# Tiles 1 and 2 as a seven-product pair for w_out, and DVE work on two units at a time

## The chip, the cores and the metric

The kernel runs on one core of a Trainium2 chip. The metric is device time in microseconds (us) for one execution, the median of several runs. The engines are TensorE (PE, with its weight loads shown apart as PEld), VectorE (DVE), ScalarE (ACT), GpSimd (POOL) and SyncE (SP); SP does no arithmetic, its queue issues most of the DMA transfers.

## The reference

Linear attention for 8 batches and 8 heads of 576 positions feeds a feed-forward layer on 4608 tokens:

```python
q_s = softmax(q, axis=-1); k_s = softmax(k, axis=2)
kv = einsum('bhsd,bhse->bhde', k_s, v)
x  = einsum('bhsd,bhde->bhse', q_s, kv)      # -> (4608 tokens, d_model 512)
g  = softplus(x @ w_in)                      # w_in 512 x 2048
out = g @ w_out                              # w_out 2048 x 512
```

All inputs and outputs are float32. The kernel keeps the accuracy by writing each operand as a sum of two float32r parts, hi and lo, and each product as three matmuls: hi*hi, lo*hi, hi*lo.

## The kernel before

**Tiles and units.** The 4608 tokens are nine tiles of 512. The 2048 columns of the hidden layer are 16 units j of 128. A tile's `w_in` product for a unit is 4 x 3 matmuls of 128x128 weights on 512 columns, its `w_out` product again 4 x 3.

**Tiles alone and tiles in pairs.** Tiles 0 to `SOLO`-1 (0, 1, 2) go alone: `up` (L743 to L745) makes one unit of `x @ w_in`, `softplus` (L752) bends it, `split_g` (L758 on ACT, L761 on DVE) makes hi and lo of it, `down` (L785 to L787) adds its share of `g @ w_out` into four PSUM banks `po0` to `po3`, `finish` stores the tile row by row from SP's queue. The other six tiles go in three pairs p. In a pair, both products are 2x2 block products done with seven block products for eight (the Strassen-Winograd scheme): `pair_unit` (L870 to L872) for `w_in`, on operands that `operand_unit` forms, and `product_out` (L984 to L986) for `w_out`. Seven for eight costs sums and differences elsewhere: sums of blocks of the weights, once, by DVE (`sum_unit`, `sum_out_unit`, one unit s, that is two columns j, at a time; kept in DRAM and fetched again), and differences of g by DVE for each pair (`less_g`, L951), then hi and lo of each of the seven right sides (`split_right`: L964 on ACT, L967 on DVE). Its results are transposed by DVE (L1021) and stored by POOL's queue, eight stores of 64 KB for every 256 columns of a tile (`store`, L1029).

**Order.** Nothing is scheduled at run time. `ORDER` is a written-out string of tokens, and every engine runs its instructions in the order in which the tokens stand: `U` up, `A` softplus, `G`, `H` split_g, `O`, `I` down, `Y` and `y` sums of weights, `C` pair_unit, `t` less_g, `e` split_right, `d` product_out, `R` and `r` fetches from DRAM, `o` the end of a pair, `k` and `q` the attention. SBUF holds some twenty slots of 8 KB a partition (`w0` to `w15`, `spare`, `x0` to `x2`, `qt`). A tile that takes a slot waits until the last reader of the tile before has done, so the table of slots sets waits too. An instruction that waits holds up what stands behind it on its engine; on SP's queue that holds for the fetches.

Of the kernel before, what the change touches and what calls it, by code (L numbers as in the profile page):

```python
# [39 lines left out]
SOLO = 3  # L40
# [4 lines left out]
IN_HOMES = {0: ("spare", "w2"), 1: ("w2", "spare"), 2: ("spare", "w2")}  # L45
# [4 lines left out]
STAGE = ("w1", "w15", "w0", "spare", "w5", "w6", "w7", "w8")  # L50
STAGE_OUT = ("w12", "w13", "w14", "w1", "w12", "w13", "x1", "w3")
# [10 lines left out]
    k1.3.3 S9 M12.1 J9 q1.6 U8 J10 G7 O7 k1.2.4 M14.1 P9 T11 k1.3.4 D3 Q9 k1.2.5 k1.2.6 M11.1 W1 k1.2.7 J11 k1.3.5 P10
    k1.3.6 q1.5 k1.3.7 U9 Q10 J12 D10 A8 P11 Q11 G8 A9 G9 U10 T15 q1.8 q1.7 k1.2.8 q1.9 P12 Q12 k1.2.9 U11 q1.10
    k1.3.8 A10 A11 O8 M13.1 G10 k2.0.0 T14 T13 J13 P13 Q13 x1.0.0 O9 q1.11 D9 J14 G11 O10 W3 D2 D12 M15.1 U12 A12 W0
    U13 x1.0.1 x1.0.2 P14 Q14 J15 D14 A13 O11 x1.0.3 U14 k1.3.9 x1.1.0 G12 P15 D5 x1.0.4 x1.0.5 A14 O12 x1.1.1 x1.1.2
    x1.1.3 G13 G14 Q15.1 P0 x1.2.0 x1.2.1 x1.2.2 O13 x1.2.3 U15 x1.1.4 x1.1.5 x1.3.0 L2 x1.3.1 x1.3.2 D4 Q0.1 k2.1.0
    x1.3.3 x1.2.4 x1.2.5 x1.3.4 D0 P1 Q1.1 x1.3.5 U16 A15 O14 D1 q2.0 q2.1 G15 k2.0.1 Y0.0 Y0.2 A16 G16 U17 U18 A17
    k2.1.1 U19 k2.0.2 k2.0.3 A18 D7 q2.2 q2.4.1 k2.1.2 k2.0.4 k2.0.5 U20 k2.1.3 k2.1.4 k2.1.5 O15 G17 A19 A20 k2.1.6
    k2.0.6 n n O16 Y0.1 G18 Y1.0 q2.6 q2.8 k2.0.7 k2.1.7 k2.1.8 U21 A21 Y1.2 k2.2.0 Y0.3 U22 O17 G19 k2.1.9 q2.3 D6
    Y1.1 k2.0.8 Y1.3 O18 G20 k2.0.9 Y3.0 k2.3.0 O19 A22 G21 O20 G22 k2.3.1 Y3.1 k2.2.1 Y3.2 Y0.4 k2.2.2 q2.5 Y2.0 Y2.1  # L70
    O21 D8 O22 k2.2.3 k2.3.2 k2.3.3 k2.3.4 k2.3.5 k2.2.4 q2.7 L3 D15 Y4.0 U23 k2.2.5 Y2.2 Y2.3 k2.3.6 k2.2.6 q2.9 A23
    H1.7.0 H1.7.1 k2.2.7 k2.3.7 U24 A24 Y2.4 Y2.5 q2.10 U25 Y4.2 O23 U26 H1.8.0 k2.2.8 k2.2.9 x2.0.0 Y1.4 H1.8.1 A25
    q3.0 x2.0.1 x2.0.2 q3.1 q3.12 H1.9.0 x2.0.3 q2.11 Y3.3 n k3.0.0 Y2.6 O24 D13 Y2.7 U27 Y3.4 k2.3.8 H1.9.1 x2.0.4
    x2.0.5 x2.2.0 k2.3.9 x2.1.0 x2.1.1 Y1.5 Y4.1 Y3.5 Y4.3 O25 A26 H1.10.0 Y4.4 n Y0.5 k3.1.0 Y3.6 A27 U28 A28 x2.1.2
    Y1.6 H1.11.0 H1.10.1 x2.1.3 O26 Y2.8 Y3.7 H1.12.0 U29 q3.2 Y6.0 q3.3 H1.11.1 x2.2.1 x2.1.4 x2.1.5 x2.3.0 D11 O27
    Y0.6 Y0.7 H1.12.1 A29 U30 k3.0.4 k3.0.5 k3.1.4 x2.2.2 q3.5 k3.1.5 Y4.5 x2.2.3 Y1.7 O28 x2.3.1 q3.4 x2.3.2 q3.6
    R0.0 H1.13.0 A30 H1.14.0 U31 Y3.8 Y4.6 x2.3.3 A31 q3.7 Y0.8 H1.13.1 L4 O29 H1.14.1 q3.8 x2.2.4 Y6.1 q3.13 R0.1
    x2.2.5 R0.2 x2.3.4 x2.3.5 k3.0.6 y0.0 y0.1 q3.9 H1.15.0 y0.2 y0.3 H1.15.1 k3.1.6 k3.0.7 k3.0.8 U32 A32 n n q4.0
# [1166 lines left out]
```

## Time and profile before

| | us |
|---|---|
| three runs | 811.52, 811.63, 814.35 |
| median | 811.63 |
| profiled execution | 812.18 |
| its span, first to last instruction | 810.1 |
| PE busy in the span | 801.4 |
| DVE, ACT, POOL busy | 623.6, 513.9, 115.1 |

"Busy" is the time in which an engine works on at least one instruction. Matmuls overlap, so the time of one (0.39 us) is longer than the distance from one to the next; PE's pace is read from the starts in the timeline. Windows give the busy time of each engine in a stretch of the span, the waits say which engine waited for which instruction, and the chain of waits follows the end of the program back to its start.

### The profile page before, as it was taken

How to read it: one execution, taken by the hardware profiler on the slowest of the kernel's cores; microseconds unless marked ns; L12 is line 12 of the kernel's file. 1: busy time of each engine (PE TensorE's matmuls, PEld its weight loads, DVE VectorE, ACT ScalarE, POOL GpSimd, SP SyncE). 2: the span in 40 equal slices, each digit the busy share in tenths (PEclk: the TensorE clock that was granted, in tenths of full speed). 3: DMA queues.
4: the chain of work that ended last, by engine and by line, in shares of the span. 5: the costliest groups of instructions: out<-in, count | busy, mean ns of one | idle time of the engine just before them, and what ended most of it. 6: DMA issues, size and time to landing. Idle time of an engine off the chain costs nothing.

```text
span 810.1 us, 12075 instructions
## 1 busy us (share of the span) xinstructions
PE 801.4 (99%) x4244; PEld 656.3 (81%) x4244; DVE 623.6 (77%) x1027; ACT 513.9 (63%) x860; POOL 115.1 (14%) x219
## 2 busy tenths in 40 slices
PE   8999999999999999999999999999999999999997
PEld 7578888888888888888888888888888888888885
DVE  8889884689899998878599998757798932228884
ACT  4999954545674846586887566676676632436552
POOL 1320022001010100100010021430000111600017
PEclk9999999999999999999999999999999999999999
DMA  9976736665798799898588477973756664839845
GB/s 344 376 266 234 267 131 234 215 214 208 253 342 310 246 371 322 315 307 300 185 266 246 146 216 269 279 248 116 240 176 192 195 208 167 264 128 291 268 118 92
DMA packets 114492, 193.74 MB, mean 239 GB/s; under 512 B 8000, under 2 KB 90176, under 8 KB 104192
## 3 DMA queue, kind: packets, MB, share of 16 engines
q1 hardware_dynamic: 111168, 186.67, 67.8%
q0 software_dynamic: 2944, 6.04, 3.7%
q8 instruction: 34, 0.56, 0.3%
q10 hardware_dynamic: 320, 0.26, 0.1%
q14 instruction: 26, 0.21, 0.1%
HBM read 149.95 MB, written 42.99 MB: 238 GB/s over the span
## 4 chain that ended last, share of the span: by engine, by line
PE 88%; DVE 4%; POOL 3%; ACT 1%; DMA 1%; issue 1%; POOLq 0%; ACTq 0%
PE po L984 6%; PE po L985 6%; PE po L986 6%; PE po L870 6%; PE po L871 5%; PE po L872 5%; PE ph L743 5%; PE po L787 5%; PE po L785 5%; PE ph L744 5%; PE ph L745 4%; PE po L786 4%; PE ph L870 3%; PE ph L872 3%; PE ph L871 3%; PE ph L984 3%
## 5 line engine op out<-in xcount | busy, mean ns | idle before, releaser
L1029 POOL DMA_DIRECT2D out<-w x92 | 59.4, 653 | 292.3 <-DVE w L1021 287.6
L743 PE MATMUL ph<-x,w 128*128 128x512 f32 x164 | 65.0, 396 | 0.0
L785 PE MATMUL po<-w,g_hi 128*128 128x512 f32 x164 | 64.7, 395 | 0.0
L787 PE MATMUL po<-w,g_lo 128*128 128x512 f32 x164 | 64.1, 391 | 0.5 <-DVE g_lo L761 0.5
L744 PE MATMUL ph<-x,w 128*128 128x512 f32 x164 | 64.0, 390 | 0.0
L786 PE MATMUL po<-w,g_hi 128*128 128x512 f32 x164 | 63.9, 390 | 0.0
L745 PE MATMUL ph<-x,w 128*128 128x512 f32 x164 | 63.9, 390 | 0.0
L967 DVE TENSOR_TENSOR g_lo<-w,g_hi 128x512 fp32r<-128x512 f32 x74 | 49.4, 682 | 16.8 <-ACT g_hi L964 16.7
L964 ACT CAST g_hi<-w 128x512 fp32r<-128x512 f32 x74 | 45.5, 620 | 19.6 <-PE po L985 16.5
L951 DVE TENSOR_TENSOR w<-w,w 128x512 f32<-128x512 f32 x72 | 48.4, 681 | 3.0 <-ACT w L904 2.0
L870 PE MATMUL po<-w,x 128*128 128x512 f32 x112 | 44.3, 395 | 0.0
L872 PE MATMUL po<-w,x 128*128 128x512 f32 x112 | 43.6, 390 | 0.0
L871 PE MATMUL po<-w,x 128*128 128x512 f32 x112 | 43.6, 389 | 0.0
L487 POOL PARTITION_ALL_REDUCE mx<-mx x20 | 19.1, 954 | 172.0 <-DVE mx L484 169.8
L964 ACT CAST w<-w 128x512 fp32r<-128x512 f32 x52 | 31.9, 620 | 17.9 <-PE po L985 13.9
L893 DVE TENSOR_TENSOR w<-po,w 128x512 f32<-128x512 f32 x24 | 16.5, 686 | 34.1 <-PE po L872 34.0
L761 DVE TENSOR_TENSOR g_lo<-g,g_hi 128x512 fp32r<-128x512 f32 x46 | 31.4, 688 | 13.7 <-ACT g_hi L758 13.5
L967 DVE TENSOR_TENSOR w<-w,w 128x512 fp32r<-128x512 f32 x52 | 35.2, 683 | 6.1 <-ACT w L964 5.9
L758 ACT CAST g_hi<-g 128x512 fp32r<-128x512 f32 x46 | 28.3, 620 | 15.6 <-PE po L786 12.8
L752 ACT ACTIVATE g<-ph 128x512 f32<-128x512 f32 x48 | 28.6, 601 | 14.7 <-PE ph L745 14.2
L787 PEld LDWEIGHTS po<-w,g_lo 128*128 128x128 f32 x164 | 30.8, 188 | 7.9 <-DVE g_lo L761 1.4
L484 DVE TENSOR_REDUCE mx<-kvt 128x128 f32<-128x640 f32 x28 | 36.8, 1324 | 0.1
(392 smaller groups left out, 2371.3 us busy)
## 6 DMA issues: line engine op xcount, KB each, us to landing
x<-sums SPq DMA_DIRECT2D x24, 1024.0 KB, 5.6
kvt<-in_kv SPq DMA_DIRECT2D x30, 512.0 KB, 6.3
kept<-w SPq DMA_DIRECT2D x15, 1024.0 KB, 7.5
w<-kept SPq DMA_DIRECT2D x13, 1024.0 KB, 7.9
x<-sums_out SPq DMA_DIRECT2D x44, 256.0 KB, 5.0
w<-kept SPq DMA_DIRECT2D x36, 256.0 KB, 4.8
x<-kept SPq DMA_DIRECT2D x36, 256.0 KB, 4.4
w<-sums_out SPq DMA_DIRECT2D x36, 256.0 KB, 5.4
```

Of the source, the lines that this page charges most:

```text
L743: nc.tensor.matmul(ph, lhsT=w_hi, rhs=x_hi, start=h == 0, stop=False)
L744: nc.tensor.matmul(ph, lhsT=w_lo, rhs=x_hi, start=False, stop=False)
L745: nc.tensor.matmul(ph, lhsT=w_hi, rhs=x_lo, start=False, stop=h == HP - 1)
L785: nc.tensor.matmul(po, lhsT=g_hi[:, ms], rhs=w_hi, start=j == 0, stop=False)
L786: nc.tensor.matmul(po, lhsT=g_hi[:, ms], rhs=w_lo, start=False, stop=False)
L787: nc.tensor.matmul(po, lhsT=g_lo[:, ms], rhs=w_hi, start=False, stop=j == NJ - 1)
L870: nc.tensor.matmul(ph, lhsT=w_hi, rhs=x_hi, start=c == 0 and i in (0, 4), stop=False, **more)
L871: nc.tensor.matmul(ph, lhsT=w_lo, rhs=x_hi, start=False, stop=False, **more)
L872: nc.tensor.matmul(ph, lhsT=w_hi, rhs=x_lo, start=False, stop=c == 1, **more)
L964: nc.scalar.copy(ring[p, i, s][0], right_of(p, i, s))
L967: engine.tensor_tensor(out=lo, in0=right_of(p, i, s), in1=hi.bitcast(F32), op=ALU.subtract)
L984: nc.tensor.matmul(bank, lhsT=w_hi, rhs=hi, start=begin, stop=False, **more)
```

## The change

`SOLO` falls from 3 to 1, so there are four pairs. The new pair 0 is tiles 1 and 2. It takes part in the seven-product scheme for `w_out` only: its `w_in` products are still made by `up`, 16 units for each tile, with g of both tiles kept in SBUF (slots `g0.1.*`, `g0.2.*`) until its `w_out` products run. The weights' hi and lo parts are kept in DRAM, and the parts for `up` of tiles 1 and 2 are fetched again two columns at a time (`fetch_w`, `part_in`).

DVE and ACT work on two units per instruction in three places: differences of g (`less_g`), hi and lo of the right sides (`split_right`, with views from `two_of`), and the sums of blocks of the weights (`sums_unit`, which takes the place of `sum_unit` and `sum_out_unit`; for `w_in` the parts are fetched from DRAM by `fetch_parts` first). The ring that holds hi and lo has six units in place of four. Slots are given out by a table, `HOMES`; `ORDER` is a new string. Tiles 1 and 2 are stored as the other pairs are, by POOL.

```diff
-SOLO = 3
+SOLO = 1
 ORDER = """
-    k1.0.3 k1.0.4 U0 k1.1.0 k1.0.5 J4 U1 A0 k1.0.6 x0.2.3 k1.0.7 x0.2.4 O0 J3 P2 Q2 x0.0.3 ...
+    k1.0.3 k1.0.4 U0 k1.0.5 k1.1.0 A0 x0.3.3 P2 x0.1.3 J4 x0.0.3 x0.2.3 J3 P3 Q2 M5 x0.0.4 ...
...
+HOMES = """
+    q0:qt kv2:x0 kv3:x2 raw0:w0 raw1:w1 raw2:w2 raw3:w3 qT:w15 x0:x1 raw4:w4 raw5:w5 ...
+    x1.0:w4 parts0:x2 parts14:w0 parts15:qt x1.1:w5 q2:w6 y0:spare y1:w11 g0.1.0:x2 ...
+    T3.2:x1 T2.2:w13 T4.2:w1 end1.3:x2 sum17:w9 g6.1.0:w7 sum18:spare g5.0.0:w3 ...
+    sum22:x2 g6.1.1:x0 sum21:spare g5.0.1:w9 g6.0.1:w6 g5.1.1:w0 ...
...
+    def slot(key, shape, dtype=F32R):
+        return wp.tile([P] + list(shape), dtype, name=HOMES[key])
...
+    gg = const.tile([P, 2, 2, TOK], F32R, name="gg")
...
+    def fetch_w(s):
+        again[s] = slot(f"again{s}", (2, 2, DM))
+        for z in range(2):
+            nc.sync.dma_start(out=again[s][:, z].bitcast(F32), in_=kept[2 * s + z][:, :, 0])
+
+    def fetch_parts(u):
+        for i in range(2):
+            pulled[u, i] = slot(f"{'YH'[i]}{u}", (2, 4, 2 * P))
...
+    def part_in(j, i):
+        return again[j // 2][:, j % 2, i] if j // 2 in again else parts[j][:, i, 0]
...
+    def sums_unit(u, side, keeps):
...
+        def whole(z=None, engine=nc.vector):
+            if side == 0:
+                engine.tensor_tensor(out=y, in0=y, in1=split[0].bitcast(F32), op=ALU.add)
+                return
...
         def add(out, a, b, op, engine=nc.vector):
-            engine.tensor_tensor(out=y[:, out], in0=y[:, a], in1=y[:, b], op=op)
+            engine.tensor_tensor(out=y[:, :, out], in0=y[:, :, a], in1=y[:, :, b], op=op)
...
     def softplus(t, j, ph):
-        soft[t, j] = tp.tile([P, TOK], F32, name="g", bufs=3)
+        if t:
+            if ("up", t, j // 4) not in state_g:
+                state_g["up", t, j // 4] = slot(f"g0.{t}.{j // 4}", (4, TOK), F32)
+            soft[t, j] = state_g["up", t, j // 4][:, j % 4]
+        else:
+            soft[t, j] = tp.tile([P, TOK], F32, name="g", bufs=3)
         nc.scalar.activation(soft[t, j], ph, AF.Softplus)
...
+    def two_of(t, j):
+        z, k = j % 2, j // 2 % 4
+        if ("up", t, j // 4) in state_g:
+            return state_g["up", t, j // 4].rearrange("p (k z) n -> p k z n", z=2)[:, :, z]
+        return state_g[t, z, j // 8][:, k:k + 2]
...
     def less_g(p, name, s, engine=nc.vector):
-        b11, b12, b21, b22 = (soft.get((t, 2 * s + z)) for z in range(2) for t in (ta, tb))
+        out, a, b = (two_of((ta, tb)[int(n[1]) - 1], 2 * s + int(n[0]) - 1) for n in (out, a, b))
         engine.tensor_tensor(out=out, in0=a, in1=b, op=ALU.subtract)
...
     def split_right(p, i, s, part, engine=nc.vector):
+            place = n // 2 % 3 + 3 * (p == NP - 1 and 0 <= n - 6 * NS < 4)
+            if place == 0:
+                t = gg
...
+            ring[p, i, s, "two"] = [t[:, :, k] for k in range(2)]
+            nc.scalar.copy(ring[p, i, s, "two"][0], right_of(p, i, s))
```

In the rows below, a name is the tile's slot and a number that the builder gives it; `x`, `w` or `spare` is the slot's family.

First PE, tile 1's first unit in `w_out` before: four banks, three matmuls each.

```order
L785 MATMUL po_1437<-w_1185,g_hi 128x512
L786 MATMUL po_1437<-w_1185,g_hi 128x512
L787 MATMUL po_1437<-w_1185,g_lo 128x512
L785 MATMUL po_1438<-w_1185,g_hi 128x512
L786 MATMUL po_1438<-w_1185,g_hi 128x512
L787 MATMUL po_1438<-w_1185,g_lo 128x512
L785 MATMUL po_1439<-w_1185,g_hi 128x512
L786 MATMUL po_1439<-w_1185,g_hi 128x512
L787 MATMUL po_1439<-w_1185,g_lo 128x512
L785 MATMUL po_1440<-w_1185,g_hi 128x512
L786 MATMUL po_1440<-w_1185,g_hi 128x512
L787 MATMUL po_1440<-w_1185,g_lo 128x512
```

And the new pair's first product of `w_out` in the changed kernel, the first unit s (`gg` is the first place of the ring, `w_2112` the block of weights fetched from DRAM):

```order
L980 MATMUL ph_2218<-gg,w_2112 128x512
L981 MATMUL ph_2218<-gg,w_2112 128x512
L982 MATMUL ph_2218<-gg,w_2112 128x512
L980 MATMUL ph_2222<-gg,w_2112 128x512
L981 MATMUL ph_2222<-gg,w_2112 128x512
L982 MATMUL ph_2222<-gg,w_2112 128x512
```

Before, two tiles and two units were four such groups of 12 matmuls, 48 in all; now they are seven groups of 6, that is 42.

Second DVE, in the first pair's `w_out` before (L967 a lo part, L951 a difference of g, L893 and L897 of the next pair's `w_in`, L677 of the attention):

```order
L967 TENSOR_TENSOR g_lo_3431<-w12_3160,g_hi_3430 128x512
L951 TENSOR_TENSOR w15_3608<-w15_3608,x1_3606 128x512
L897 TENSOR_TENSOR w3_3756<-po2_3669,g_3604 128x512
L677 TENSOR_TENSOR q_lo_3797<-att1_108,q_hi_3796 128x512
L893 TENSOR_TENSOR w0_3574<-po3_3758,w0_3574 128x512
```

And in the new pair's `w_out` in the changed kernel (L944 a difference, L963 the lo part, L493 the maximum of the attention's k):

```order
L963 TENSOR_TENSOR gg_106<-x0_1714,gg_106 128x2x512
L963 TENSOR_TENSOR w4_2161<-w5_1805,w4_2161 128x2x512
L944 TENSOR_TENSOR w5_1805<-w5_1805 128x2x512
L963 TENSOR_TENSOR w10_2245<-w8_1937,w10_2245 128x2x512
L944 TENSOR_TENSOR x2_1368<-w5_1805,x2_1368 128x2x512
L944 TENSOR_TENSOR w8_1937<-w8_1937 128x2x512
L686 TENSOR_TENSOR q_lo_2333<-att1_102,q_hi_2332 128x512
L493 TENSOR_REDUCE mx_2377<-kvt_2257 128x128
```

Each instruction now covers two units, 1024 elements a partition.

Third POOL in the changed kernel, where the pair of tiles 3 and 4 is stored (`x2_4598` and `w0_4239` hold its transposed results, L496 is the maximum across partitions, L467 to L470 fill a k tile):

```order
L1026 DMA out_0<-w0_4239 32x16x32 x4
L1026 DMA out_0<-x2_4598 32x16x32 x12
L467 MEMSET kvt_4763 64x2x64
L468 MEMSET kvt_4763 64x2x65
L470 MEMSET kvt_4763 128x10
L496 ISA mx_4785<-mx_4783 128x128
L1026 DMA out_0<-w0_4239 32x16x32 x8
L1026 DMA out_0<-x2_4598 32x16x32 x4
L1026 DMA out_0<-w0_4239 32x16x32 x4
```

And SP's queue there: `x2_4995` takes the slot that `x2_4598` leaves, and holds the sums of weights for the next pair's seventh unit of `w_in`.

```order
L403 DMA w14_3995<-kept12_1299 128x2x512
L415 DMA x2_4995<-sums0_6_3589 128x2048
L403 DMA w14_3995<-kept14_1419 128x2x512
L471 DMA kvt_5026<-in_kv 128x8x128
L475 DMA kvt_5026<-in_kv_tail 64x2x128
L415 DMA spare_5077<-sums0_7_3839 128x2048
```

Before, the slots that the stores of a pair emptied were written next by ACT or DVE; here one is filled by a fetch, which stands in SP's queue ahead of the others.

## Rows read from the trace of the kernel before

**Rows 1.** The page: busy time by engine, and PE's granted clock by slice.

```profile
PE 801.4 (99%) x4244; PEld 656.3 (81%) x4244; DVE 623.6 (77%) x1027; ACT 513.9 (63%) x860; POOL 115.1 (14%) x219
...
PEclk9999999999999999999999999999999999999999
```

**Rows 2.** Waits of PE, whole span: total us, times, longest.

```profile
PE ph L1186 <- DVE ident L268: 3.0, 1, 3.0
PE po L1044 <- DVE w L1037: 0.5, 1, 0.5
PE po L787 <- DVE g_lo L761: 0.5, 2, 0.4
```

**Rows 3.** Timeline of PE: start us, us of one, instruction.

```profile
121.94 0.40 PE L743 MATMUL ph<-x,w 128*128 128x512 f32 x1
122.17 0.39 PE L744 MATMUL ph<-x,w 128*128 128x512 f32 x1
...
123.99 0.39 PE L743 MATMUL ph<-x,w 128*128 128x512 f32 x1
```

**Rows 4.** DVE by form: shape and count | busy us, mean ns | idle before.

```profile
L951 DVE TENSOR_TENSOR w<-w,w 128x512 f32<-128x512 f32 x72 | 48.4, 681 | 3.0 <-ACT w L904 2.0 <-ACT w L900 0.7
L400 DVE TENSOR_TENSOR w<-w 128x512 f32<-128x512 f32 x13 | 8.7, 683 | 0.0
L409 DVE TENSOR_TENSOR w<-w 128x1024 fp32r<-128x1024 f32 x7 | 8.5, 1214 | 0.9 <-ACT w L406 0.9
L403 DVE TENSOR_TENSOR w<-w 128x256 f32<-128x256 f32 x28 | 11.6, 418 | 0.3
L1021 DVE STREAM_TRANSPOSE w<-w 128x512 f32<-128x512 f32 x23 | 16.1, 703 | 2.3 <-ACT w L1004 2.1
```

**Rows 5.** ACT by form, the same columns.

```profile
L964 ACT CAST g_hi<-w 128x512 fp32r<-128x512 f32 x74 | 45.5, 620 | 19.6 <-PE po L985 16.5 <-PE ph L985 1.4 <-DVE g_lo L967 0.8
L406 ACT CAST w<-w 128x1024 fp32r<-128x1024 f32 x7 | 7.3, 1048 | 0.0
```

**Rows 6.** Windows: length, PE, PEld, DVE, ACT, POOL busy (count), PEclk, DMA share, GB/s.

```profile
200.00:250.00 50.00, 49.72 (x291) 40.70 (x290) 44.99 (x77) 31.93 (x56) 3.70 (x14) 1.00 0.83 294
250.00:300.00 50.00, 49.64 (x299) 41.07 (x298) 45.24 (x80) 31.82 (x52) 6.50 (x16) 1.00 0.82 297
300.00:350.00 50.00, 50.00 (x261) 41.47 (x260) 41.13 (x67) 31.99 (x58) 3.27 (x8) 1.00 0.92 316
400.00:450.00 50.00, 50.00 (x273) 40.98 (x272) 47.47 (x80) 40.23 (x75) 3.11 (x11) 1.00 0.80 248
450.00:500.00 50.00, 50.00 (x229) 41.79 (x228) 48.28 (x76) 27.42 (x51) 7.53 (x10) 1.00 0.60 187
```

**Rows 7.** Timeline of POOL: start us, us, instruction [idle before, releaser].

```profile
490.57 1.06 POOL L487 PARTITION_ALL_REDUCE mx<-mx  x1 [7.53 <-DVE mx L484]
...
517.61 0.70 POOL L487 PARTITION_ALL_REDUCE mx<-mx  x1 [3.87 <-DVE mx L484]
518.19 6.41 POOL L1029 DMA_DIRECT2D out<-w  x10
...
536.07 0.66 POOL L1029 DMA_DIRECT2D out<-w  x1 [1.37 <-DMA out<-w]
...
790.80 15.38 POOL L1029 DMA_DIRECT2D out<-w  x24 [7.55 <-DVE w L1021]
```

**Rows 8.** Chain of waits, 505 to 545 us: start us, us, what.

```profile
521.39 6.03 DMA out<-w
...
530.26 5.04 DMA out<-w
535.30 0.59 ACT w L890
...
539.32 0.50 ACT po L882
539.87 0.50 PE po L870
```

**Rows 9.** POOL by form, and DVE's idle time behind it.

```profile
L519 DVE TENSOR_TENSOR kvt<-kvt,mx 128x640 f32<-128x640 f32 x20 | 16.3, 818 | 4.0 <-POOL mx L487 3.9
...
L487 POOL PARTITION_ALL_REDUCE mx<-mx x20 | 19.1, 954 | 172.0 <-DVE mx L484 169.8 <-PE ph L872 1.7 <-PE ph L986 0.6
```

**Rows 10.** DMA: issues, KB each, median us from issue to landing.

```profile
x<-sums SPq DMA_DIRECT2D x24, 1024.0 KB, 5.6
...
out<-w POOLq DMA_DIRECT2D x92, 64.0 KB, 4.1
...
out<-w SPq DMA_DIRECT2D x2, 128.0 KB, 3.0
```

**Rows 11.** Timeline at the end: PE's last product, the last issues.

```profile
804.06 0.39 PE L986 MATMUL po<-x,spare 128*128 128x512 f32 x1
804.48 0.75 DVE L1037 TENSOR_SCALAR w<-po 128x256 f32<-128x256 f32 x2 [4.10 <-PE po L986]
...
805.79 0.93 SPq L1052 DMA_DIRECT2D out<-w  x2
```

More of the change, by code (lines that the diff above doesn't have):

```diff
@@ L62 @@
[L62 to L66, printed above, removed]
@@ L203 @@
+"""
+HOMES = dict(entry.split(":") for entry in HOMES.split())
 assert START[-1] == NT
@@ L349, in split_w @@
         if part == 0:
-            parts[k] = wp.tile([P, 2, 2, DM], F32R, name=f"w{(k - 1) % NJ}" if k != UNSPLIT % NJ else "spare")
+            parts[k] = slot(f"parts{k}", (2, 2, DM))
         hi, lo = (parts[k][:, i].rearrange("p z n -> p (z n)") for i in range(2))
@@ L387, in fetch_sums @@
         s = n % NS
-        sums_w[s] = xp.tile([P, 2, 4, 2 * P], F32R, name=f"x{2 - 2 * (n % 2)}")
-        nc.sync.dma_start(out=sums_w[s].bitcast(F32), in_=kept_sums[s])
-    def sum_unit(s):
-        f = wp.tile([P, 2, 4, 2 * P], F32R, name=STAGE[s])
-        y = f[:, 1].bitcast(F32)
-        old = parts[2 * s + 1], parts[2 * s]
-        def whole_w(z, engine=nc.vector):
-            hi, lo = (old[z][:, i, 0].bitcast(F32) for i in range(2))
-            engine.tensor_tensor(out=y[:, 2 * z:2 * z + 2].rearrange("p a n -> p (a n)"), in0=hi, in1=lo, op=ALU.add)
+        t = slot(f"sum{n}", (2, 4, 2 * P))
@@ new lines, in fetch_sums @@
+        sums_w[s] = t[:, 0], t[:, 1]
+        nc.sync.dma_start(out=t.bitcast(F32), in_=kept_sums[s])
+    def sums_unit(u, side, keeps):
+        y = (pulled[u, 0] if side == 0 else slot(f"y{u}", (2, 4, 2 * P))).bitcast(F32)
+        split = [pulled[u, 1]] if side == 0 else []
+        def whole(z=None, engine=nc.vector):
+            if side == 0:
+                engine.tensor_tensor(out=y, in0=y, in1=split[0].bitcast(F32), op=ALU.add)
+                return
+            hi, lo = (parts[4 * u + z][:, i, 1].bitcast(F32) for i in range(2))
+            first = 2 * (z % 2)
+            out = y[:, z // 2, first:first + 2].rearrange("p a n -> p (a n)")
+            engine.tensor_tensor(out=out, in0=hi, in1=lo, op=ALU.add)
@@ new lines, in high, with low, keep @@
+            if side:
+                split.append(slot(f"h{u}", (2, 4, 2 * P)))
+            nc.scalar.copy(split[0], y)
+        def low(engine=nc.vector):
+            split.append(slot(f"{'Yy'[side]}l{u}", (2, 4, 2 * P)))
+            engine.tensor_tensor(out=split[1], in0=y, in1=split[0].bitcast(F32), op=ALU.subtract)
+            if side == 0:
+                for z in range(2):
+                    sums_w[2 * u + z] = split[0][:, z], split[1][:, z]
+        def keep(z):
+            t = keeps[2 * u + z] = dram.tile([P, 2, 4, 2 * P], F32, name=f"sums{side}_{2 * u + z}")
+            for i, f in enumerate(split):
+                nc.sync.dma_start(out=t[:, i], in_=f[:, z].bitcast(F32))
@@ L449, in tile_attn_ffn, with kv_load @@
+        steps = (((1, 0, 1, ALU.add), (0, 2, 0, ALU.subtract), (2, 1, 2, ALU.subtract), (3, 3, 2, ALU.subtract)),
+                 ((3, 1, 3, ALU.add), (1, 0, 1, ALU.subtract), (0, 3, 0, ALU.subtract), (2, 2, 0, ALU.subtract)))[side]
+        return [lambda *e, a=a: add(*a, *e) for a in steps] + [
+            high, low, lambda: keep(0), lambda: keep(1)
+        ] + [lambda *e, z=z: whole(z, *e) for z in range(4)]
     KVW = 2 * D + 1
-    def kv_load(b, h, engine=nc.gpsimd, queue=nc.sync, pool=kp, tag="kvt", shape=(P, NCH + 1, 2, KVW)):
-        t, w = pool.tile(list(shape), F32, name=tag), KVW if b else 2 * D
+    def kv_load(b, h, engine=nc.gpsimd, queue=nc.sync):
+        wide, w = not b and h >= 2, KVW if b else 2 * D
+        t = slot(f"kv{h}", (HP * TOK,), F32) if wide else kp.tile([P, NCH + 1, 2, KVW], F32, name="kvt")
@@ L1064, in tile_attn_ffn @@
     kv_order = [(b, h) for b in range(B) for h in range(HP)]
[L1065 to L1072 removed]
+    loaded, ahead = {}, [0]
     def kv_prefetch(**place):
```

489 lines of the change are left out of this document (215 added, 274 removed).

## The prediction

> **What bounds the kernel now.** I read four views in this order. The page's busy times: PE works 801.4 of the 810.1 us, DVE comes next with 77%, and PE's granted clock is full in every slice [rows 1]. But matmuls overlap, so a busy PE says little by itself; the timeline gives the pace. From the start at 121.94 to that at 123.99 lie nine 128x512 matmuls, 0.228 us each, although one lasts 0.39 us [rows 3]; over the whole trace I take 0.2275. Third, the waits: all that the view finds for PE is one wait of 3.0 us at the start, 0.5 us at the end and 0.5 us twice summed in the middle [rows 2]. The reader is to see that after the start PE issues one matmul after the other and hardly ever waits. Fourth, the windows, for how near the others are: DVE is busy 48.28 and 47.47 of 50 us between 400 and 500, and PE loses nothing there; between 200 and 300 DVE has 45 of 50 and PE loses 0.28 and 0.36 us [rows 6]. So **PE's issue bounds the kernel**, and DVE stands right behind it. A matmul less is a gain as long as DVE keeps up.
>
> **PE, what goes.** Before, tiles 1 and 2 need 2 x 16 x 12 = 384 matmuls in `down`. The new pair needs 7 products x 8 units s x 6 = 336. Counted in the built programs, 128x512 matmuls fall from 3152 to 3104, and no other form changes: 48 x 0.2275 = **10.9 us** [rows 3]. All of it lies on the path, since PE hardly waits. That the change does not do what it says is excluded by this count.
>
> **DVE, what is added.** Merging saves little: two 512-element instructions last 2 x 0.68 = 1.37 us and one of 1024 lasts 1.214 [rows 4], but neighbours on DVE overlap by 0.048 us each (the durations of all 1029 instructions sum to 673, DVE is busy 623.6), so a merged pair gains 0.1 us. What is new is pair 0: differences, more lo parts and eight transposes. By form, with durations of [rows 4]: 512-element tensor_tensor 500 to 188 (-312 x 0.683 = -213.1), 1024 from 61 to 221 (+160 x 1.216 = +194.6), 256 from 64 to none (-26.9), sums of 2x256 none to 32 (+21.9), transposes +8 (+5.6), four more adds (+2.7), and twelve of 2048 elements, a form that the trace does not have. From 512 to 1024 an instruction grows by 0.533 us, so 2.28 us is my estimate for 2048, +27.4; ends: 2.0 and 2.43 (two of 1024). Sum +12.2; with 160 instructions fewer the overlap shrinks by 7.7, so DVE goes from 623.6 to **643.5 us**, from 77% to 80.5% of a shorter span.
>
> The mean hides the place. I laid DVE's instructions against PE's in the order of the built program and summed both by these durations. Between 100 and 450 us of PE's work DVE had 306 us of work before; it has **339 us of 350** now, 96.8%, because `up` of two tiles in a row, pair 0's differences and all sums of weights fall there. In its fullest part, 200 to 280 us of PE's work, DVE has 4.8 us more than PE; the fullest part before had 3.8 more. So DVE must be kept at 96.8% for 350 us where it showed 97% for 100 us [rows 6]. If it holds 96%, this stretch takes 339/0.96 = 352.8 us, so PE waits **2.8 us**; that is the value I take, near the two windows. The ends: nothing if it holds 97%, and 25 us at the 90% of the windows between 200 and 300 [rows 6], which I hold for far off, since DVE there was not asked for more.
>
> **A rule weighed.** The all-reduce on POOL took 0.70 us once and 1.06 another time [rows 7], and DVE idled 3.9 us behind twenty of them [rows 9]. The Trainium skill, "SBUF — State Buffer", Who interferes with whom, says that a DVE instruction with two SBUF inputs keeps a GpSimd instruction that reads SBUF out for as long as it lasts. By that rule these all-reduces wait up to 1.2 us instead of 0.7 for a merged instruction, and DVE's idle time grows by 3.9 x (1.216/0.683 - 1) = 3.0 us in the very stretch that has none to spare: the sum below would be 807.1. The trace shows the longer times, not what they hang on.
>
> **ACT.** Casts of 512 fall from 300 to 100 (-200 x 0.62), 112 of 1024 come (+112 x 1.05), 16 of 1024 go, eight of 2048 come (estimate 1.9 from the two rows), two copies and two table loads: -4 us of 513.9 [rows 1, 5]. It stays at 64%; cost nothing, hidden under PE.
>
> **DMA and SP's queue.** SP issues 494 transfers for 406; bytes go from 192.9 to 199.2 MB. Between 50 and 250 us of PE's work the order issues 15 to 16 MB per 50 us, some 310 GB/s. The chip moved 294 to 316 GB/s for 150 us with the DMA share at 0.82 to 0.92, and PE lost 0.6 us there [rows 6]. In the order a refetched `w_in` part is issued 8 to 35 us of PE's work ahead of its first matmul, blocks of weights 4 us or more as before, against landings of about 5.6 us for a megabyte [rows 10]. I take nothing; if the cover fails, one late megabyte costs 2 to 5 us.
>
> **The added wait.** `x2_4995`, sums for the next pair's `w_in`, goes into the slot that the stores of tiles 3 and 4 empty. SP's queue stands at this fetch until POOL's stores from `x2_4598` have landed; behind it wait a `w_in` part and the next k tile, and PE's matmul on `x2_4995` stands right after it. Before, such a backlog ran 24 stores in 536.73 - 518.19 = 18.5 us, 0.77 us each [rows 7], landings took 5.0 to 6.0 us, and ACT's copy came late by it, with PE right behind [rows 8]. Now: all-reduce 0.7, twelve stores 9.2, landing 5.5, the fetch 5.6 [rows 10] make 21.0 us, and between the all-reduce and the matmul lie 20.0 us of PE's work. **1.0 us** of wait; ends 0 (stores at 0.64 us, landing 4.1: 18.1 us) and 4.
>
> **The end.** Before, POOL's last 24 issues run to 806.18 [rows 7], 1.9 us behind PE's last matmul at 804.3, and land at 810.1. In the new order POOL's last issue comes by the same 0.64 us a store 0.9 us behind it, so the end passes to SP's two stores, issued till 806.7 and landing after 3.0 [rows 10, 11]: 809.7. **0.4 us** less.
>
> **Sum.** Against the profiled span, 810.1 - 10.9 + 2.8 + 1.0 - 0.4 = 802.6. The median of the runs is 811.63, 1.5 us over that span (the profiled run's own time is 812.18), so the median will be **804.1 us**.
>
> **The rivals.** (a) **DVE takes the gain back.** The price goes by one number, the share at which DVE can be kept from 100 to 450 us: 95% costs PE 6.5 us and gives 807.8, 93% costs 14 and gives 815.6. For it: in the rows DVE idles behind ACT and PE (3.0 us before L951 [rows 4]), and a merged instruction starts only when both units are there. Against it: 97% in [rows 6], and a ring of six units for four. This ends within 0.5% of before. (b) **Slower**, the same mechanism past its point: below 92.8% the stretch grows by more than 15 us and the time passes 815.7. At 92% it is 811.6 - 10.9 + 18.2 + 1.0 - 0.4 = 819.5. (c) **The lock of the all-reduce**: 807.1 by the rule above, as a mechanism of its own. (d) **DVE costs nothing**: it holds 97% and the fetch is not late, 811.63 - 10.9 - 0.4 = 800.3; for it speaks that PE's loss between 400 and 500 was nil.
>
> **How the numbers follow.** 0.5%, about what a measurement of this kernel can tell from no change, is 4.1 us: faster is below 807.6, slower above 815.7. Forecast, 802 to 806: 0.48. (d), 799.5 to 802: 0.18. (c), 806 to 807.6: 0.10. (a), 807.6 to 815.7: 0.17. (b): 0.07. Faster is 0.76, no change 0.17, slower 0.07. The range goes from 800.0 to 810.0: it leaves out the lower edge of (d), (b), and the upper part of (a), not quite 0.2 in all.
>
> **What will show it.** PE's 128x512 matmuls still 0.2275 us apart; PE's waits, about 4 us more, on DVE's lo parts and differences (L963, L944) between 140 and 490 us; DVE at 96% or more in the windows there; one wait of PE on L872, or of SP, at the fetch of `x2` near 535 us; twelve DVE instructions of 2048 elements at 2.28 us. I am wrong if DVE stays under 94% in those windows while PE waits for it, if PE waits for DMA landings between 100 and 300 us, or if the 48 matmuls are gone and the span is not shorter by more than 5 us.

## The result, and the profile after

| | before | after |
|---|---|---|
| median, us (four runs each) | 812.99 (811.52 to 814.62) | 804.97 (804.63 to 805.22) |
| span of the profiled execution, us | 810.1 | 802.8 |
| matmul records | 4244 | 4196 |

The ratio is 0.9901, 95% interval 0.9875 to 0.9926: faster by 8.0 us, 1.0%. The forecast was 804.1, its range 800.0 to 810.0; by the span it was 802.6, and 802.8 is measured. The sum, though, is right by luck in one part: two errors in it cancel, and that is what the experiments are about.

The page of the kernel after (answers to [rows 1]):

```profile
PE 794.0 (99%) x4196; PEld 647.0 (81%) x4196; DVE 645.7 (80%) x867; ACT 514.8 (64%) x768; POOL 138.1 (17%) x251
...
PEclk9999999999999999999999999999999999999999
```

PE's waits, whole span, after (answers to [rows 2]: total us, times, longest):

```profile
PE ph L1175 <- DVE ident L282: 3.0, 1, 3.0
PE ph L872 <- ACT ph L882: 0.7, 1, 0.7
PE att L692 <- DVE q_lo L686: 0.6, 1, 0.6
PE po L1041 <- DVE g L1034: 0.5, 1, 0.5
```

There is no wait on DVE's lo parts or differences (L963, L944), where I had put 2.8 us, and none at the fetch of `x2`, where I had put 1.0. Two short waits that I had not foreseen stand in their place. The windows after (answers to [rows 6], same columns) show DVE's load:

```profile
100.00:225.00 125.00, 125.00 (x673) 103.49 (x672) 109.88 (x160) 91.74 (x135) 13.07 (x25) 1.00 0.86 295
225.00:314.00 89.00, 89.00 (x506) 73.34 (x505) 86.64 (x110) 53.94 (x79) 12.69 (x29) 1.00 0.86 259
314.00:450.00 136.00, 135.34 (x706) 111.13 (x705) 125.99 (x156) 95.61 (x152) 21.77 (x44) 1.00 0.85 269
```

DVE is busy 109.9 + 86.6 + 126.0 = 322.5 of the 350 us, 92%, and for the 89 us of the new pair's `w_out` 97.3%; PE loses nothing in these 89.

So 10.9 us of matmuls went, PE waited hardly more than before, and yet the span is only 7.3 shorter. The missing part shows in the timeline, at the end of the last product (the columns of [rows 3]):

```profile
795.17 0.39 PE L982 MATMUL po<-w,w 128*128 128x512 f32 x1
795.40 0.39 PE L980 MATMUL po<-w,w 128*128 128x512 f32 x1
795.62 0.39 PE L981 MATMUL po<-w,w 128*128 128x512 f32 x1
795.85 0.39 PE L982 MATMUL po<-w,w 128*128 128x512 f32 x1
796.08 0.40 PE L980 MATMUL po<-gg,w 128*128 128x512 f32 x1
796.31 0.40 PE L981 MATMUL po<-gg,w 128*128 128x512 f32 x1
796.55 0.40 PE L982 MATMUL po<-gg,w 128*128 128x512 f32 x1
796.78 0.40 PE L980 MATMUL po<-gg,w 128*128 128x512 f32 x1
797.01 0.40 PE L981 MATMUL po<-gg,w 128*128 128x512 f32 x1
797.25 0.40 PE L982 MATMUL po<-gg,w 128*128 128x512 f32 x1
```

Matmuls on slots start (796.08 - 795.17)/4 = 0.2275 us apart, those on `gg`, the first place of the ring, (797.25 - 796.08)/5 = 0.234. No engine waits and the clock is full, so no view of waits names it. Over the whole trace, the 636 matmuls with `gg` as moving operand (the 512 columns that stream through) or as weights (the 128x128 block that stays) go at 0.2333 us on average, all other 128x512 ones at 0.2275.

### The profile page after: what moved, and what is told of

It is laid out like the page before. It is cut to its first block, busy times and chain, and to the rows that moved or that the text cites. A ratio compares the mean times of both kernels' runs of the same rounds, so it can differ in the third digit from the quotient of the medians.

```text
span 802.8 us, 11782 instructions
## 1 busy us (share of the span) xinstructions
PE 794.0 (99%) x4196; PEld 647.0 (81%) x4196; DVE 645.7 (80%) x867; ACT 514.8 (64%) x768; POOL 138.1 (17%) x251
## 4 chain that ended last, share of the span: by engine, by line
PE 93%; DVE 3%; DMA 1%; issue 1%; ACT 1%; SPq 0%; DVEq 0%; ACTq 0%
PE po L980 9%; PE po L981 9%; PE po L982 9%; PE po L872 6%; PE po L873 6%; PE po L874 6%; PE ph L752 5%; PE ph L754 5%; PE ph L753 5%; PE ph L980 4%; PE ph L981 4%; PE ph L982 4%; PE ph L872 4%; PE ph L873 3%; PE ph L874 3%; PE att L544 2%
## 5 line engine op out<-in xcount | busy, mean ns | idle before, releaser
L960 ACT CAST w<-w 128x1024 fp32r<-128x1024 f32 x50 | 52.2, 1049 | 33.7 <-PE po L981 18.7
L1026 POOL DMA_DIRECT2D out<-x x60 | 38.6, 651 | 201.0 <-DVE x L1018 198.2
L963 DVE TENSOR_TENSOR w<-w,w 128x1024 fp32r<-128x1024 f32 x50 | 60.8, 1221 | 8.3 <-ACT w L960 8.1
L944 DVE TENSOR_TENSOR w<-w,w 128x1024 f32<-128x1024 f32 x46 | 55.7, 1218 | 3.7 <-DMA w<-kept 2.6
L496 POOL PARTITION_ALL_REDUCE mx<-mx x20 | 20.4, 1018 | 179.7 <-DVE mx L493 178.5
L1026 POOL DMA_DIRECT2D out<-w x64 | 41.5, 656 | 56.1 <-DVE w L1018 56.0
L980 PE MATMUL po<-w,w 128*128 128x512 f32 x128 | 50.4, 393 | 0.0
L981 PE MATMUL po<-w,w 128*128 128x512 f32 x128 | 49.9, 390 | 0.0
L873 PE MATMUL po<-w,w 128*128 128x512 f32 x128 | 49.9, 390 | 0.0
L982 PE MATMUL po<-w,w 128*128 128x512 f32 x128 | 49.8, 389 | 0.0
L960 ACT CAST gg<-w 128x1024 fp32r<-128x1024 f32 x33 | 34.6, 1050 | 20.9 <-PE po L981 8.5
L893 DVE TENSOR_TENSOR x<-po,x 128x512 f32<-128x512 f32 x12 | 8.3, 692 | 49.3 <-PE po L874 49.3
L963 DVE TENSOR_TENSOR gg<-w,gg 128x1024 fp32r<-128x1024 f32 x33 | 40.3, 1222 | 5.5 <-ACT gg L960 5.4
L872 PE MATMUL po<-w,w 128*128 128x512 f32 x110 | 43.1, 392 | 0.0
L874 PE MATMUL po<-w,w 128*128 128x512 f32 x110 | 42.8, 389 | 0.0
L493 DVE TENSOR_REDUCE mx<-kvt 128x128 f32<-128x640 f32 x28 | 36.7, 1324 | 5.2 <-DMA kvt<-in_kv_tail 5.1
L752 PE MATMUL ph<-w,w 128*128 128x512 f32 x98 | 39.4, 402 | 0.0
L753 PE MATMUL ph<-w,w 128*128 128x512 f32 x98 | 38.2, 390 | 0.0
L754 PE MATMUL ph<-w,w 128*128 128x512 f32 x98 | 38.2, 389 | 0.0
L467 POOL MEMSET kvt<- 64x128 f32 x28 | 5.7, 203 | 164.0 <-PE att L544 44.9
L873 PE MATMUL ph<-w,w 128*128 128x512 f32 x80 | 31.2, 390 | 0.0
L980 PE MATMUL po<-gg,w 128*128 128x512 f32 x76 | 30.2, 397 | 0.0
```

The source lines that it names most:

```text
L752: nc.tensor.matmul(ph, lhsT=w_hi, rhs=x_hi, start=h == 0, stop=False)
L753: nc.tensor.matmul(ph, lhsT=w_lo, rhs=x_hi, start=False, stop=False)
L754: nc.tensor.matmul(ph, lhsT=w_hi, rhs=x_lo, start=False, stop=h == HP - 1)
L872: nc.tensor.matmul(ph, lhsT=w_hi, rhs=x_hi, start=c == 0 and i in (0, 4), stop=False, **more)
L873: nc.tensor.matmul(ph, lhsT=w_lo, rhs=x_hi, start=False, stop=False, **more)
L874: nc.tensor.matmul(ph, lhsT=w_hi, rhs=x_lo, start=False, stop=c == 1, **more)
```

## Experiments: why matmuls on `gg` are slow

`gg` is new: one constant tile of 8 KB a partition, laid out behind a 4-byte tile, in place of four small ones. My first theory was its address, 32 bytes past a multiple of 64.

**e1_gg_at_64**

```diff
+    gg = const.tile([P, 2, 2, TOK], F32R, name="gg")
     one = const.tile([P, 1], F32, name="one")
-    gg = const.tile([P, 2, 2, TOK], F32R, name="gg")
```

> The changed kernel with one line moved: the tile gg is laid out ahead of the 4-byte tile one, so that it begins at byte 25728 of a partition, a multiple of 64, and no longer 32 bytes past one; every other large tile stays where it was, and no instruction changes. In the trace of the changed kernel the 636 matmuls of 128x512 that read gg, as moving operand or as weights, start 0.2333 us apart and the others mostly 0.2267. Theory A, the place of gg costs this: with it moved, those matmuls go at 0.2267 us, 636 x 0.0066 = 4.2 us go, 805.0 becomes 800.8 (bounds 800.2 to 801.6). Rival B, it is what gg is (a tile that ACT and DVE write while PE reads its other half): pace and time stay, 805.0, within 0.5. Rival C, the pace changes but DVE is the bound where gg is read (DVE 97% busy from 225 to 314 us): PE waits for DVE instead and less than half of it comes, 803 to 805.

804.84 us, and moving reads of `gg` still 0.2333 us apart. Only its reads as weights went down, to 0.2294. **e2_before_at_32** moved everything in the kernel before by 32 bytes:

```diff
-        first = const.tile([P, 1], F32, name="first")
+        first = const.tile([P, 9], F32, name="first")[:, 0:1]
```

> The kernel before with a 4-byte tile of its start laid out 36 bytes long: all slots, parts and halves of g move on by 32 bytes, from a multiple of 64 to 32 bytes past one; no instruction changes. Theory A, a 128x512 matmul that reads from such a place takes 0.0066 us more: 3150 x 0.0066 = 21 us if weights and moving operand together cost it once (813 becomes 834, bounds 831 to 838), 42 us if each costs it by itself (855). Rival B, nothing of the place: 813.

813.17 against 812.44, ratio 1.0005 (0.9996 to 1.0014): no change. The theory of the single address has fallen. Three more kernels moved `gg`, or all else, elsewhere: **e5_gg_at_64_of_128**, **e6_all_at_0_of_128** and **e9_gg_far**.

```diff
e5, with first padded to 96 bytes:
+    gg = const.tile([P, 4 * TOK + 16], F32R, name="gg")[:, 16:].rearrange("p (a b n) -> p a b n", a=2, b=2)
     one = const.tile([P, 1], F32, name="one")
e6: as e1, and
+        first = const.tile([P, 24], F32, name="first")[:, 0:1]
e9:
+    gg = sm.tile([P, 2, 2, TOK], F32R, name="gg")
```

> The changed kernel with gg alone moved by 32 bytes, to byte 25792 of a partition, 64 past a multiple of 128, where all other slots lie too (64 past a multiple of 128, as before). With gg at 25728, a multiple of 128, its moving reads stayed at 0.2333 us and its reads as weights fell to 0.2294 on average. Theory A2, what counts is the place within 128 bytes (64 and 96 are quick, 0 and 32 slow) or that moving operand and weights lie alike in it: all 636 go at 0.2267, 804.9 becomes 800.7 (800 to 802). Rival B, gg is slow for another reason than its address (x1 lay at this very byte in the kernel before and was read at 0.2270): no change, 804.8.

> The changed kernel with gg at byte 25728, a multiple of 128, and all other large tiles moved by 64 bytes to multiples of 128 as well. Theory A2 in the absolute form (0 past a multiple of 128 is a slow place): all 128x512 matmuls go at 0.2333, 2500 more than now, +16 us, 821. In the relative form (moving operand and weights have to lie alike): all are quick, 801. Rival B, the address says nothing: 804.8.

> The changed kernel with gg laid out among the last tiles of a partition, at byte 218432 (64 past a multiple of 128) instead of 25760; all slots move down by 8192 and keep their alignment. Alignment is out by the runs before: with gg at 0, 32 and 64 past a multiple of 128 its 636 matmuls stayed at 0.2325 to 0.2333 us on average, although the pattern of single values changed. Theory A3, it is the stretch of memory in which gg lies (about 25 to 34 KB): gg goes at 0.2270 and 4 us go, 800.5 to 801.5; what lies there now (g, a part of qt) becomes slow where PE reads it. Rival B2, it goes with gg wherever it lies: pace 0.2325 or more and 804.7.

804.54, 804.41 and 804.67: `gg` stayed slow everywhere, so each theory of a place fell. But the single values repeated. In e5, e6 and e9 the starts fell into the same groups (0.224, 0.229, 0.234, 0.237 to 0.238), although `gg` lay at three addresses and two alignments. What these three share is, up to its sign, the distance from `gg` to the slots that hold the other operand. Worked out for every 128x512 matmul from the addresses of the built programs, as the address of the moving operand less that of the weights, modulo 512:

```
kernel   gg moving: distance, us apart   gg as weights: distance, us apart   all at distance 0
before   -                               -                                   0.2273
e2       -                               -                                   0.2274
after    480  0.2334                     32   0.2333                         0.2275
e1       448  0.2333                     64   0.2294                         0.2275
e5, e6   384  0.2326                     128  0.2326                         0.2275
e9       128  0.2326                     384  0.2325                         0.2275
```

All slots, and before the four tiles of g too, lie multiples of 2048 bytes apart, so distance 0 was the rule without anybody's care (but for 12 matmuls of the attention, at 64). e5 did not move `gg` alone, as its expectation has it: the two paddings moved all slots too, by 128 bytes, and so it missed distance 0. Two kernels test the new theory from both sides: one brings `gg` into step, the other puts the kernel before out of step.

**e11_gg_in_step** (with the two moves of e7, below, whose own time is 803.76)

```diff
-    gg = const.tile([P, 2, 2, TOK], F32R, name="gg")
+    gg = tp.tile([P, 2, 2, TOK], F32R, name="gg")
```

> The changed kernel with the two moves of the order that took PE's waits at 96 and 314 us away (803.8 by themselves), and gg in front of the three tiles g, at byte 25792: from it to each of the slots is now a multiple of 512 bytes. Over the traces so far, the 128x512 matmuls whose moving operand and weights lie a multiple of 512 bytes apart go at 0.2273 us on average, and those that lie 32, 64, 128, 384, 448 or 480 past one at 0.229 to 0.234, whatever the place itself; before, all lie in step. Theory E, only this distance counts: the 636 matmuls on gg go at 0.2273, 636 x 0.0060 = 3.8 us go, 799.9 (799.2 to 800.6). Rival B2, it is gg itself: pace 0.2325 or more, 803.0 to 803.8.

**e12_before_apart**

```diff
+        tp.tile([P, 8], F32, name="pad")
```

> The kernel before with an empty tile of 32 bytes laid out between the tiles x0 to x2, g_hi and g_lo on one side and the slots w0 to w15, spare and qt on the other; no instruction changes. 2232 matmuls of 128x512 have one operand on each side, so that their distance is 32 or 480 past a multiple of 512 instead of none. Theory E: these 2232 take 0.0061 us more each, 13.6 us, 826 (824 to 828). Rival B2, gg was slow for something of its own: 812.5.

e11 takes **799.73 us** (799.60 to 800.38), 4.0 less than e7, ratio to before 0.9839 (0.9825 to 0.9853): faster than both kernels. e12 takes **824.96** against 813.02, ratio 1.0147 (1.0133 to 1.0162), 11.9 us for an empty tile of 32 bytes. Timeline of e11 at the end:

```profile
791.37 0.39 PE L980 MATMUL po<-gg,w 128*128 128x512 f32 x1
791.60 0.39 PE L981 MATMUL po<-gg,w 128*128 128x512 f32 x1
...
792.51 0.39 PE L982 MATMUL po<-gg,w 128*128 128x512 f32 x1
```

and of e12, in `down`, where the operands of a matmul lie on either side of the empty tile:

```profile
127.79 0.40 PE L785 MATMUL po<-w,g_hi 128*128 128x512 f32 x1
128.03 0.39 PE L786 MATMUL po<-w,g_hi 128*128 128x512 f32 x1
128.26 0.40 PE L787 MATMUL po<-w,g_lo 128*128 128x512 f32 x1
128.49 0.39 PE L785 MATMUL po<-w,g_hi 128*128 128x512 f32 x1
128.73 0.40 PE L786 MATMUL po<-w,g_hi 128*128 128x512 f32 x1
128.96 0.39 PE L787 MATMUL po<-w,g_lo 128*128 128x512 f32 x1
```

From the first to the sixth of its matmuls `gg` goes at (792.51 - 791.37)/5 = 0.228 us in e11, the operands put apart in e12 at (128.96 - 127.79)/5 = 0.234. Over the whole traces, e11 has 0.2272 with `gg` moving and 0.2278 with `gg` as weights; e12 has 0.2332 for the operands put apart, which before went at 0.2274. In e11 `gg` begins at the very byte at which it began in e5, 25792; the slots lie otherwise, by 128 bytes, and the pace is 0.2272 in place of 0.2326. The two moves of e7 are not the reason, for in e7 `gg` still goes at 0.2333 to 0.2335. The distance between the operands is shown as the cause, by prediction in both directions.

The 11.9 us are less than the 13.6 forecast, and the distance within one matmul is not the whole account. By the starts in e12's trace the matmuls put apart take 12.6 us more; PE's gaps cost 1.6 less; and some 870 matmuls whose own operands stayed in step got slower too, from 0.2269 to 0.2294, 2.2 us in all. Part of this stands right behind matmuls that are out of step: the first five of such a run take (441.39 - 440.23)/5 = 0.232 us each:

```profile
440.23 0.39 PE L984 MATMUL po<-w,w 128*128 128x512 f32 x1
...
441.39 0.39 PE L986 MATMUL po<-w,w 128*128 128x512 f32 x1
```

Why the chip minds the distance, why it lingers, whether it counts to a matmul's own weights or to those of the next one, and whether 512 is the exact period, stays open: distances 32, 64, 128, 384, 448 and 480 were tried, others not.

## Experiments: how near DVE is

The question that carried most of my doubt: what does PE pay when DVE gets more to do in the stretch from 225 to 314 us, or PE less?

**e3_lo_twice**

```diff
+            for _ in range(2 if p == 0 and s % 4 == 0 else 1):
                 engine.tensor_tensor(out=lo, in0=right_of(p, i, s), in1=hi.bitcast(F32), op=ALU.subtract)
```

> The changed kernel in which DVE makes 14 of the 28 lo parts of pair 0 twice, with the same result: 14 x 1.22 = 17 us more DVE work (16.4 without the overlap of neighbours) between 225 and 314 us, where DVE is busy 86.6 of 89 us and PE never waits. Theory D, DVE is within 3% of being the bound there: only some 2.4 us and its lead on PE are free, and PE waits for 8 to 14 us on L980; 813 to 819, with DVE at 99% or more in that stretch before PE waits at all. Rival (cover): DVE runs far enough ahead, PE waits for less than 3 us, 805 to 808. Rival (a) of the prediction, that DVE can't be kept above 93 to 95%: the extra work is paid in full, 821 or more.

819.78 us, 14.8 more for 16.4 us of added DVE work. Its windows:

```profile
225.00:245.00 20.00, 20.00 (x125) 16.47 (x124) 19.04 (x26) 10.89 (x19) 0.93 (x6) 1.00 0.88 269
245.00:265.00 20.00, 16.75 (x107) 12.85 (x106) 19.80 (x21) 9.93 (x14) 3.90 (x8) 1.00 0.83 252
265.00:285.00 20.00, 16.97 (x77) 13.39 (x76) 19.67 (x25) 10.48 (x16) 3.36 (x2) 1.00 0.62 179
```

DVE reaches 99% while PE drops to 84%: DVE can be kept at 98 to 99%, well above the 93 to 95% of rival (a), and 90% of what is added is paid, so that some 1.6 us of it were free. The time lies just above the 813 to 819 that I gave: DVE's lead on PE, from which I took a part, was nearly nothing.

**e8_48_less**

```diff
-            nc.tensor.matmul(bank, lhsT=w_hi, rhs=lo, start=False, stop=s == NS - 1, **more)
+            if not (p == 0 and i in TURN[:4] and s < 6):
+                nc.tensor.matmul(bank, lhsT=w_hi, rhs=lo, start=False, stop=s == NS - 1, **more)
```

> The changed kernel with 48 matmuls fewer in pair 0 (the hi*lo matmul of the first six units in four of the seven products of w_out is left out, so the rows of tiles 1 and 2 lack that share); all DVE and ACT work stays. They stand where DVE is busy 86.6 of 89 us and PE does not wait. Theory D, DVE is the next bound there: 89 - 10.9 = 78 us of PE work against 86.6 of DVE work, so 2.4 us and what lead DVE has come back, 800 to 802.5, and PE waits for DVE on L980 or L982. Rival: a matmul less still gains its 0.2275 us, 794.

805.74 us (804.67 to 806.20): 48 matmuls less and nothing gained, 0.8 us lost by the medians. Its waits of PE (lines from 982 on stand one further down), and its windows:

```profile
PE ph L983 <- DVE gg L963: 3.9, 2, 3.2
PE po L983 <- DVE w L963: 3.0, 2, 1.8
```

```profile
265.00:275.00 10.00, 6.79 (x29) 5.30 (x29) 10.00 (x10) 4.16 (x6) 2.24 (x2) 0.86 0.68 227
275.00:285.00 10.00, 10.00 (x73) 8.11 (x72) 8.53 (x10) 4.75 (x9) 0.74 (x5) 0.80 0.82 257
```

```profile
269.47 0.40 PE L981 MATMUL ph<-gg,w 128*128 128x512 f32 x1
273.08 0.80 PE L983 MATMUL ph<-gg,w 128*128 128x512 f32 x1 [3.21 <-DVE gg L963]
273.67 0.63 PE L980 MATMUL ph<-gg,w 128*128 128x512 f32 x1
274.10 0.63 PE L981 MATMUL ph<-gg,w 128*128 128x512 f32 x1
```

PE waits 6.9 us for DVE's lo parts. In its longest wait, 3.2 us to 273.08, the granted clock falls from 2.4 to 1.2 GHz; the two windows have a mean of 0.86 and 0.80, where the kernel after had 1.00. The 14 matmuls from 273.08 us on start 0.43 us apart in place of 0.23, which costs 2.8 us. From start to start, between 228.6 us and the seam to the next pair, PE's waits for DVE cost 8.2 us more than in the kernel after, the low clock 2.8, and the smaller matmuls 1.4: 12.4 us, against the 10.9 that went. Theory D, which expected 800 to 802.5, had the waits and left out the clock. So DVE is the bound in this stretch, and 48 matmuls less there bring no gain; smaller numbers were not tried.

**e4_one_unit**: lo parts and differences in two instructions of 512 elements each (these lines are the differences; the lo parts are done likewise).

```diff
-        engine.tensor_tensor(out=out, in0=a, in1=b, op=ALU.subtract)
+        for z in range(2):
+            engine.tensor_tensor(out=out[:, z], in0=a[:, z], in1=b[:, z], op=ALU.subtract)
```

> The changed kernel with the merge undone on DVE alone: each difference of g (L944) and each lo part (L963) is made by two instructions of 512 elements instead of one of 1024; ACT's casts stay at two units. Two of 0.683 us less the overlap of 0.048 each for one of 1.216 less 0.048: +0.10 us for each of 154 merged instructions, +15 us of DVE, some 3 us of it between 225 and 314 us, where 2.4 are free. Theory: the merge is worth nearly nothing on DVE: 805 to 806.5. Rival: merged instructions carry the change, and PE waits for most of what is added: 810 or more.

806.25 us, 1.3 more, as the theory had it. DVE's page shows 655.6 us busy and 1043 instructions, +9.9 us for 176 more, 0.06 us each, not my 0.10. Merging on DVE is worth little, but where DVE is at 97% even that reaches the time: start by start, PE falls 0.6 us behind the kernel after near 291 us, with one new wait on a lo part, and some 0.25 at the seam. Another 0.4 are lost at 10 us, where nothing was changed.

## Experiments: the two new waits

At 89.50 us POOL makes a lo part of weights (L369) while DVE runs L659. Timeline of the kernel after, POOL, DVE and PE:

```profile
89.50 3.37 POOL L369 TENSOR_TENSOR w<-w,w 128x1024 fp32r<-128x1024 f32 x1 [3.18 <-ACT w L367]
...
89.37 4.58 DVE L659 TENSOR_TENSOR qt<-qt,s 128x1024 f32<-128x1024 f32 x2
...
97.40 0.30 PE L692 MATMUL att<-q_hi,kv_hi 128*128 128x64 f32 x1 [0.61 <-DVE q_lo L686]
```

Two DVE instructions take 4.58 us, where one takes 1.22 elsewhere, and POOL's takes 3.37 beside 2.45 elsewhere. They take turns: the first L659 (1.21 us) ends at 90.58, POOL's at 92.87, and the second L659, started at 90.49, ends at 93.95. At the end of DVE's chain PE waits 0.6 us. The other wait, at 314 us, is the seam between two pairs: PE's second product of the next pair needs ACT's copy L882 of the first, and nothing stands between them on PE.

**e7_two_waits**

```diff
-    ... Q1.1 ...
+    ... Q1 ...
-    ... d0.6.7 C1.0.0 ... o0.c21.1 ... C1.0.7 C1.0.1 ...
+    ... C1.0.0 d0.6.7 ... C1.0.7 o0.c21.1 ... C1.0.1 ...
```

> The changed kernel with two moves in the order. The lo part of weights that POOL makes at 89.5 us (L369, 3.37 us beside a DVE instruction L659 that takes 3.46 there and 1.22 elsewhere) goes to DVE; PE's wait of 0.6 us on q_lo at 96 us hangs on that instruction. And at 314 us, where PE waits 0.7 us for ACT's copy L882, the last six matmuls of pair 0 in w_out are put behind the first product of the next pair, and ACT's L882 ahead of its L1001. Theory: both waits go, 804.9 becomes 803.6. Rival: the waits come back as others (DVE carries 1.2 us more, the copies L1001 come later): 804.9.

803.76 us, 1.2 less (by the profiled spans 0.8); both waits are gone from its list, as expected. **e10_both** joined these moves with the far `gg` of e9, both edits as above:

> The same, with the two moves of the order that took away PE's waits at 96 and 314 us (803.8 by themselves). Theory A3: 803.8 - 4.2 = 799.6. Rival B2: 803.7.

803.02 us: the theory of the stretch of memory fails here as in e9. Of the 0.7 below e7 the distance explains 636 x (0.2333 - 0.2326) = 0.4 us; the rest is not explained.

## Why the prediction was right, and where it was not

- **PE's term, -10.9: right.** 4244 - 4196 = 48 matmuls went, and the pace of those on slots is still 0.2275. It came back in full because PE hardly waits.
- **What I left out: the pace is not one number.** I carried 0.2275 of [rows 3] over to all matmuls of the changed kernel. 636 of them read a tile that had moved, and took 0.006 us more: **+3.8 us**, the largest term after the first, and the 4.0 of e11 measure it. That 0.2275 would stay everywhere was a term put at nothing without a reason. The diff shows the tile (`gg = const.tile`); I had read it for its size alone.
- **DVE's size: right in total, wrong against PE.** Forecast 643.5 us, measured 645.7; the 2048-element instruction, estimated at 2.28, takes 2.27 to 2.30 by form:

```profile
L441 DVE TENSOR_TENSOR w<-w,w 128x2048 fp32r<-128x2048 f32 x3 | 6.9, 2297 | 1.0 <-PE ph L754 1.0
```

- The step that failed is the 96.8% from 100 to 450 us. It is a sum of durations, in which neighbours overlap by 0.048 us, set against busy times of windows [rows 6], in which they don't; I had taken the overlap off the total, but not there. After the change, the durations in that stretch sum to 344.9 us, the time in which DVE is busy is 322.5: in like terms 92%, and the **+2.8 us** was nothing. The sign that I had named, 96% or more in the windows, holds for the shorter stretch of 225 to 314 us, at 97.3%, and even there PE did not wait. Two slips beside it: [rows 6] show 96.6% and 94.9% between 400 and 500 us, not 97% for 100 us; and 339/0.96 is 353.1, not 352.8.
- **The fetch of `x2`: +1.0 was 0**, the lower end. SP did stand at it, 4.4 us, and fetched at 529.88; landing took 4.7 to 4.8, and PE's matmul came at 540.21, 5.6 us after that. The stores took 0.65 us each, not the 0.77 of [rows 7]. First the instructions of line 415 (ns, least, median and most), then the timeline of SP and PE:

```profile
L415 SPq EVENT_SEMAPHORE  x6: 17/28/4426, 525.2 to 536.1; - x6
```

```profile
529.88 0.33 SPq L415 DMA_DIRECT2D x<-sums  x1
...
540.21 0.48 PE L872 MATMUL ph<-w,x 128*128 128x512 f32 x1
```

- **The end, -0.4: right.** From the start of PE's last product to the end of the span it was 810.1 - 804.06 = 6.0 us, now 802.8 - 797.25 = 5.55.
- **ACT at 64% and DMA at nothing: right**, though ACT is busy 514.8 us where I had 509.9; between 100 and 450 us the DMA share is 0.85 to 0.86, and no wait of PE hangs on a landing.
- **In sum**: 810.1 - 10.9 + 3.8 (`gg`) + 1.3 (two new waits) - 0.5 (the two waits on L761 in [rows 2], gone) - 0.5 (end) = 803.3; the span is 802.8. I had added 3.8 us of waits that didn't come, and missed 3.8 and 1.3 that did; that these are of one size is luck. The other 0.7 of the 0.9 us between 804.1 and 804.97 lie between span and median, 1.5 us by forecast and 2.2 measured.
- **Rival (a) and (b)**: not near by the share (DVE holds 97 to 99%), but near by the distance: of the 16.4 us that e3 added to DVE only some 1.6 were free. **Rival (c)**: the rule shows itself, without a price. Behind a DVE instruction of 2048 elements the all-reduce took 2.60 us instead of 0.70, and at 271.05 us, behind two merged ones in a row, 2.67, more than the 1.2 that I had put (timeline of POOL and DVE, and DVE by form with its idle time last):

```profile
328.70 0.70 POOL L496 PARTITION_ALL_REDUCE mx<-mx  x1 [1.72 <-DVE mx L493]
330.04 2.60 POOL L496 PARTITION_ALL_REDUCE mx<-mx  x1 [0.64 <-DVE mx L493]
...
329.74 2.33 DVE L441 TENSOR_TENSOR w<-w,w 128x2048 fp32r<-128x2048 f32 x1
```

```profile
L528 DVE TENSOR_TENSOR kvt<-kvt,mx 128x640 f32<-128x640 f32 x20 | 16.4, 823 | 0.0
```

  The all-reduce rose to a mean of 1018 ns from the 954 of [rows 9], but DVE's idle time behind it went from 3.9 us to 0.0, since in the new order other work stands between. The Trainium skill, "SBUF — State Buffer", Who interferes with whom, agrees on the lock; what I added, that the lock's time is DVE's idle time, was wrong. **Rival (d)**, DVE costs nothing, was right about DVE: e11, with `gg` in step and the two new waits gone, has a span of 798.2 us, and 810.1 - 10.9 - 0.4 is 798.8.

## What to carry to other kernels

When tiles move, the pace of matmuls is part of the change: read it for each operand tile from the timeline, and keep moving operand and weights a multiple of 512 bytes apart, which one stray tile of 32 bytes can undo (e12). Compare busy times only with busy times, and look for the tight stretch with the edges of the stage, not in even windows. Before taking out more work of the bounding engine, ask what the next one has left there: here 48 further matmuls less gave nothing.

## What was not expected of the hardware

The distance effect: 0.2273 us between starts at distance 0, 0.229 to 0.234 at six other distances, wherever the two operands lay; 11.9 us of 813 in e12. The Trainium skill, "SBUF — State Buffer", Who interferes with whom, gives TensorE two independent read ports, one for the moving operand and one for weights, and says that it waits for no other engine. By that neither operand's place would matter to the other; e11 and e12 show that it does, and the measurement decides. The other: a DVE and a POOL instruction with two SBUF inputs each that meet at 89.50 us cost both engines, as they take turns: 3.37 us on POOL for 2.45, and 3.46 on DVE for 1.22.
